# New issue orders for a one-core attention and gated-MLP kernel, with later loads of w_in's second half and of w_sp, and output block 12 in two column halves

## Chip, cores and metric

One NeuronCore of a Trainium2 chip. The metric is the device time of one execution in microseconds (us); lower is better. Times are medians of several runs.

## What is computed

Two pre-layernorm blocks on one sequence of 2048 tokens of width 448, in bf16. Attention has 16 heads of 28 and looks back over 8 positions, every second token. The second block gates one half of a hidden layer of 1792 with the other half, which is mixed over tokens by a 2048 x 2048 matrix.

```python
h  = x + A(layernorm(x));  h2 = h + B(layernorm(h))
def A(x):   # H=16, Dh=28, W=8, dilation 2
    q, k, v = split(x @ wqkv)
    logits = einsum('bhsd,bhswd->bhsw', q, k[idx]) * Dh**-0.5   # idx = s - 2*w, masked below 0
    return einsum('bhsw,bhswd->bhsd', softmax(logits), v[idx]) @ wo
def B(x):   # Fh = 896
    z = gelu(x @ w_in);  z1 = z[..., :Fh];  z2 = layernorm(z[..., Fh:])
    g = einsum('ts,bsf->btf', w_sp, z2) + b_sp[None, :, None]
    return (z1 * g) @ w_out
```

## The kernel before

Tokens are cut into 16 blocks of 128. A unit u is the pair of blocks u and u+8: both halves of the sequence lie on the two halves of TensorE's rows, so a "pair" of matmuls (s = 0, 1) runs side by side and takes two PSUM banks, one each. PSUM has eight banks, so at most four such pairs are in use.

Every piece of work is a named task, and the program is written from these:

- `bn1_b`, `rs1_u`, `nrm1_b`: layernorm 1 of a block or unit (L663 to L690). For units 0 to 2 a PE transpose `tT1_u` and an eviction `ev1_u` (L697 to L710) bring the result into `xh`; for units 3 to 7 a DMA transpose `tD1_u` on SP's queue does (L692). `bn2`, `rs2`, `nrm2`, `tD2_u` are the same for layernorm 2, all eight by DMA. They share the ring `tring` of four slots.
- `dp`, `rp` (L764, L650): the q and k weights, spread to the layout that the heads need. `mmq`/`mmk` and `evq`/`evk` (L807): q and k in three chunks of tokens; chunk 2 covers units 4 to 7, so `mmq2` and `mmk2` need `tD1_4` to `tD1_7`.
- nine attention tiles i of 114 tokens: `mmv` (L847) and `evv`; `mml` (L882, 64 small matmuls in four tasks); `exp` (ACT, L895); `mask` (DVE, L902); `mmr` (row sums, L911); `ln` and `rex` (ACT, L919 and L941); `mmo` (L931, 64 small matmuls); `ot` (DVE, L949). `mmo` waits for `ln` of its tile. Two tiles can hold an `E` buffer.
- per unit: `mmy` (output projection, L985), `h` (residual, L993), layernorm 2, `mmz2` (L1005, two halves k), gelu `ge` (L1027 or L1030; units 0 to 2 are first copied by `zr`), statistics `bn3`, `ag3`, `rs3` and `nrm3` (L1052).
- `mmz1_ch_f` and `gz1` (L1068, L1078): the other half of the hidden layer; needs `win0`, the second half of `w_in`. `win1` feeds `mmz2`. Each half comes as four DMAs on ACT's queue (L578).
- `g_tc_f` (L1105): the mixing over tokens, 16 matmuls of 512 columns; the first three (`g0_0` to `g0_2` in the orders) are cut into eight parts of two matmuls. They read `wsp0_b` (tokens 0 to 1023) or `wsp1_b`, transposed by DMA on SP's queue (L966). `ua`, `um` (DVE, L1115 and L1123) add the bias and multiply by z1; `wo_m` (L1134), `oa_m` (L1142) and the store `st_m` (L1146) finish a block.

The order on each engine and on SP's and ACT's DMA queues is a list written out in `ORDER` (L39 to L92). `Planner.run` walks the five lists with estimated durations; its clock decides which PSUM bank, ring slot or buffer a task gets, and where a table load is inserted: whenever a task asks for another activation table than the one loaded (L344). Waits are then derived from the data. `chain` (L1152) adds real waits that pace DMAs: load n of a list waits for step n-1 of another list. For w_in the chain is planned only (`False`); its place in ACT's list sets its issue.

```python
1160  chain(t_win[1] + t_win[0], [t_xh[NU - 1]] * 8, False)
1161  pace = [by[n % i] for i in range(4, NT) for n in ("exp%d_0", "mask%d", "ot%d")]
1163  chain([t_wsp[b][0] for b in S_ORDER], pace, depth=2)
1166  later = [t_bb, t_wout] + [t_wsp[b][1] for b in S_ORDER]
1167  chain(later, pace, depth=2)
```

The second `pace` (L1164) is ge4 to ge7, both halves, then the gz1_1 and ua0 tasks. So of `later`, w_out waits for ge4_0, wsp1_0 for ge4_1, wsp1_8 for ge5_0, wsp1_1 for ge5_1, wsp1_9 for ge6_0, and so on. `S_ORDER` is 0 8 1 9 ... 7 15.

Of the kernel before, what the change touches and what calls it, by code (L numbers as in the profile page):

```python
# [6 lines left out]
D = 448  # L7
# [33 lines left out]
        xhalo x0 x3 x11 x10 x1 x2 wqk1 x9 x14 x6 x7 x12 x13 x15 wv0 tD1_3 x4 x5 tD1_6 tD1_7 tD1_5 tD1_4 wsp0_0 wsp0_8  # L41
        tD2_0 wsp0_1 wsp0_2 wsp0_9 tD2_2 wsp0_10 tD2_1 tD2_3 wsp0_3 wsp0_11 wsp0_12 tD2_4 tD2_5 tD2_7 tD2_6 wsp0_13
        wsp0_4 bb wsp0_5 wsp0_6 wsp0_14 w_out wsp1_8 wsp0_15 wsp1_0 wsp0_7 wsp1_9 wsp1_10 wsp1_1 wsp1_2 wsp1_3 wsp1_4
        wsp1_11 wsp1_12 wsp1_5 wsp1_13 wsp1_6 wsp1_7 wsp1_14 wsp1_15 st1 st6 st7 st2 st5 st0 st3 st4 st10 st9 st8 st11
        st15 st13 st14 st12
""",
    "pool": """
        c_ident c_V c_nhalf c_mband c_kpad c_dup rs1_3 c_ones rs1_1 rs1_2 rs1_6 rs1_7 rs1_5 rs1_4 c_wo0 rs2_0 rs2_1
        rs2_2 rs2_3 rs2_4 rs2_5 rs2_7 rs2_6 rs3_5 rs3_2 rs3_1 rs3_3 rs3_0 rs3_7 rs3_6 rs3_4
""",  # L50
    "dve": """
        c_warm c_eps c_wkp c_xpad c_wqp bnh bn1_8 bn1_0 nrmh nrm1_0 bn1_3 nrm1_8 bn1_11 bn1_10 evh bn1_1 bn1_9 bn1_2
# [12 lines left out]
""",
    "act": """
        x8 wqk0 rsh rs1_0 wv1 rpk1 rpk0 rpk2 ev1_0 rpk3 rpq0 rpq1 rpq2 evk0_0 evk0_2 evq0_0 evq0_2 ev1_1 exp0_0 exp0_1
        evk1_3 evv0 evk1_2 evq1_2 ln0 rex0 evq1_1 evq1_0 evq1_3 wo1 evk1_0 wo3 win1_00 exp1_0 exp1_1 wo0 exp2_0 ln1
        exp2_1 evk2_0 wo2 rex1 win1_04 evk2_3 exp3_0 exp3_1 ln2 win1_10 ln3 rex3 rex2 evq2_0 win1_14 exp4_0 exp4_1
        win0_00 exp5_0 evv6 ln4 exp5_1 evv4 rex4 ln5 evv5 win0_04 exp6_0 rex5 exp6_1 zr0_1 exp7_0 ln6 exp7_1 evv8  # L70
        win0_10 rex6 ln7 rex7 exp8_0 exp8_1 win0_14 zr0_0 ln8 tab rex8 zr1_0 ge0_0 zr2_1 ge0_1 ge2_0 zr1_1 ge3_0 ge3_1
        ge1_0 gz1_0_1 ge1_1 gz1_0_5 gz1_0_4 ge2_1 gz1_0_0 ge5_0 ge5_1 gz1_0_6 ge4_0 ge7_0 ge4_1 gz1_0_2 gz1_1_5 ge6_1
        gz1_1_0 ge7_1 ge6_0 gz1_0_3 gz1_1_6 gz1_1_4 gz1_1_1 gz1_1_3 gz1_1_2
""",
    "pe": """
        warm dpk1 dpk0 tTh dpq0 dpk2 tT1_0 dpq1 dpk3 dpq3 mmk0_0 dpq2 mmk0_2 mmq0_0 mmq0_2 tT1_2 tT1_1 mml0_00 mml0_01
# [12 lines left out]
        g3_3_0 wo1_0 g3_2_0 g2_6_0 g3_0_0 g3_5_0 g2_4_0 g2_2_0 wo7_0 g2_3_0 wo5_0 wo6_0 g3_1_0 g2_0_0 wo0_0 wo3_0
        g2_1_0 wo4_0 g2_5_0 g3_6_0 wo10_0 wo8_0 wo9_0 wo11_0 wo15_0 wo13_0 wo13_6 wo15_6 wo14_0 wo14_6 wo12_0 wo12_6  # L90
# [128 lines left out]

class Task:  # L220
    __slots__ = ("name", "eng", "dur", "emit", "deps", "prio", "acq", "rel", "mode", "epoch",
                 "gate", "nbytes", "start", "end", "succ", "ndep", "rt", "nmm", "alts", "bw", "waits", "mark", "soft")

    def __init__(self, name, eng, dur, emit, deps=(), prio=0.0, acq=(), rel=(), mode=None,
# [14 lines left out]
        self.bw = 215.0  # L239
        self.waits = []  # L240
# [9 lines left out]
class Planner:  # L250
# [54 lines left out]
    def run(self, setup=1.6, t0=0.7):  # L305
# [15 lines left out]
        for _ in range(len(self.tasks)):  # L321
# [53 lines left out]
def bass_sequential_preLN__sliding_local_dilated__mixer_gmlp__prompt_kernel(  # L375
# [18 lines left out]
    with contextlib.ExitStack() as top:  # L394
# [816 lines left out]
```

The softmax here doesn't subtract the row's maximum and nothing guards it: scores larger than these inputs give would overflow.

## Time and profile before

| | |
|---|---|
| median of 5 runs | 258.35 us (257.66 to 258.9) |
| the profiled execution | 258.9 us, span 257.1 us |
| mean granted TensorE clock | 0.98 of full |
| start: PE's first matmul of weights (L764) | 7.18 us |
| first dense matmuls (L807) | 11.49 us |
| first mmz1 (L1068) | 104.5 us |
| first g (L1105) | 136.42 us |
| last matmul ends, span ends | 254.3 us, 257.1 us |
| landing of the 13 DMA transposes of tring | 2.9 to 7.4 us, median 3.2 |
| landing of the 32 wsp0 and wsp1 | 3.0 to 6.6 us, median 4.1 |
| landing of the 8 parts of w_in | 4.1 to 7.0 us, median 4.9 |

The span is from the first to the last instruction of the profiled execution; the time has some 1.8 us around it. In the chain of waits each piece is the work, or the transfer, that released the next. The slices cut the span into 40 equal parts of 6.43 us. A line of the program stands for all tasks that it emits (L650 and L652 are helpers for copies on ACT and DVE). "Busy" of PE counts a stretched run of matmuls as busy.

### The profile page before, as it was taken

The page shows a single profiled execution, that of the slowest core. Times are in us where ns is not written, and L with a number is a line of the kernel's source. Part 1 is how long each engine was busy: PE and PEld are TensorE (multiplying, and loading weights), DVE is VectorE, ACT ScalarE, POOL GpSimd, SP SyncE. Part 2 cuts the span into 40 slices and gives each one's busy share as a digit, 9 for nine tenths or more (in the row PEclk, how much of TensorE's full clock was granted, in tenths as well). Part 3 has the DMA queues.
Part 4 walks back from the last instruction along what each step waited for, and adds up shares of the span by engine and source line. Part 5 has one row for each costly group of instructions (what it writes and reads, how often), then busy time and mean ns, then how long its engine had stood idle before and what let it go on. Part 6 is the DMA issues. An engine that isn't in the chain of part 4 may idle for free.

```text
span 257.1 us, 6475 instructions
## 1 busy us (share of the span) xinstructions
PE 243.7 (95%) x2906; PEld 122.1 (47%) x2917; DVE 144.5 (56%) x281; ACT 89.7 (35%) x105; POOL 28.4 (11%) x72
## 2 busy tenths in 40 slices
PE   6899979989998899999999999999999999999995
PEld 2485543445565544444444444444444444444452
DVE  7986763676887877997695012055510204423753
ACT  3878644564865876776744000000000000000000
POOL 5403400001020102110723000000000000000000
PEclk9689997999999999999999999999999999999999
DMA  6970790234693955369999920005100000010112
GB/s 210 260 106 6 130 172 6 74 74 96 117 174 79 112 113 105 71 89 193 225 194 177 186 39 0 3 0 96 27 3 18 0 0 0 16 58 0 54 62 85
DMA packets 55412, 22.03 MB, mean 86 GB/s; under 512 B 46664, under 2 KB 55256, under 8 KB 55384
## 3 DMA queue, kind: packets, MB, share of 16 engines
q1 hardware_dynamic: 51952, 16.79, 36.1%
q10 hardware_dynamic: 3432, 4.82, 7.9%
q8 instruction: 23, 0.38, 0.7%
q14 instruction: 5, 0.04, 0.1%
HBM read 8.39 MB, written 1.84 MB: 40 GB/s over the span
## 4 chain that ended last, share of the span: by engine, by line
PE 86%; DMA 5%; ACT 4%; DVE 3%; issue 1%; ACTq 0%
PE psum L1105 37%; PE psum L807 11%; PE psum L1134 8%; PE psum L1068 8%; PE psum L1005 8%; PE psum L985 4%; PE psum L882 3%; PE psum L847 3%; DMA xh<-tring 3%; DMA z2p<-in_A_wqkv_dram 2%; PE psum L931 2%; ACT reg L650 2%; ACT reg L895 1%; PE psum L911 1%; DVE reg L902 1%; DVE reg L949 1%
## 5 line engine op out<-in xcount | busy, mean ns | idle before, releaser
L1115 DVE TENSOR_TENSOR ub<-psum,reg 128x512 bf16<-128x512 f32 x28 | 18.7, 687 | 58.7 <-PE psum L1105 58.4
L1105 PE MATMUL psum<-reg,z2p 128*128 128x512 bf16 x218 | 48.8, 379 | 0.3
L1105 PE MATMUL psum<-wspT_lo,z2p 128*128 128x512 bf16 x219 | 48.1, 379 | 0.4 <-issue 0.2
L1105 PEld LDWEIGHTS psum<-wspT_lo,z2p 128*128 128x128 bf16 x224 | 21.8, 98 | 26.6 <-DVE z2p L1052 0.4
L1105 PEld LDWEIGHTS psum<-reg,z2p 128*128 128x128 bf16 x224 | 21.9, 98 | 26.1
L807 PE MATMUL psum<-xh,reg 64*128 64x128 bf16 (+3 forms) x336 | 29.6, 330 | 2.1 <-DMA xh<-tring 1.9
L650 ACT ACTIVATE reg<-psum 128x896 bf16<-128x896 f32 (+5 forms) x26 | 20.8, 840 | 7.9 <-PE psum L807 5.2
L1005 PE MATMUL psum<-w_in,xh 64*128 64x448 bf16 x224 | 22.7, 349 | 0.5 <-DVE reg L949 0.5
L895 ACT ACTIVATE reg<-psum 128x928 bf16<-128x928 f32 x18 | 17.0, 944 | 15.9 <-PE psum L847 7.1
L1134 PE MATMUL psum<-reg 128*128 128x448 bf16 x112 | 22.3, 352 | 0.1
L1068 PE MATMUL psum<-xh,w_in 64*128 64x512 bf16 x196 | 21.8, 376 | 0.0
L807 PEld LDWEIGHTS psum<-xh,reg 64*128 64x128 bf16 x336 | 14.8, 104 | 12.6 <-DMA xh<-tring 2.0
L669 DVE BATCH_NORM_STATS2 st<-x_tm 128x6 f32<-128x448 bf16 x32 | 19.4, 607 | 1.0 <-DMA x_tm<-in_A_x_dram 0.9
L1142 DVE TENSOR_TENSOR tring<-psum,x_tm 128x448 bf16<-128x448 f32 x16 | 9.8, 621 | 18.0 <-PE psum L1134 18.0
L1036 DVE BATCH_NORM_STATS2 st<-z2p 128x6 f32<-128x448 bf16 x32 | 17.7, 610 | 3.9 <-ACT z2p L1030 3.9
L656 POOL TENSOR_TENSOR rs<-rs,nhalf 128x2 f32<-128x2 f32 x23 | 17.0, 738 | 2.0
L652 DVE CAST reg<-psum 128x1024 bf16<-128x1024 f32 (+3 forms) x11 | 12.0, 1095 | 9.1 <-PE psum L807 7.5
L655 POOL TENSOR_SCALAR rs<-mv 128x2 f32<-128x2 f32 x23 | 5.5, 239 | 105.2 <-DVE mv L670 86.4
L1078 ACT ACTIVATE reg<-psum 128x1024 bf16<-128x1024 f32 x14 | 13.9, 1025 | 7.4 <-PE psum L1068 7.4
L1134 PEld LDWEIGHTS psum<-reg 128*128 128x128 bf16 x112 | 11.0, 98 | 10.6
L902 DVE TENSOR_TENSOR reg<-reg,mband 128x1856 bf16<-128x1856 bf16 x9 | 10.1, 1125 | 9.8 <-ACT reg L895 9.8
L1005 PEld LDWEIGHTS psum<-w_in,xh 64*128 64x128 bf16 x224 | 10.6, 94 | 10.4 <-DVE reg L949 0.6
(68 smaller groups left out, 214.1 us busy)
## 6 DMA issues: line engine op xcount, KB each, us to landing
w_in<-in_B_w_in_dram ACTq DMA_DIRECT2D x4, 448.0 KB, 5.6
out_dram<-tring SPq DMA_DIRECT2D x16, 112.0 KB, 1.7
x_tm<-in_A_x_dram SPq DMA_DIRECT2D x15, 112.0 KB, 5.2
w_in<-in_B_w_in_dram ACTq DMA_DIRECT2D x4, 336.0 KB, 4.3
reg<-in_B_w_out_dram SPq DMA_DIRECT2D x1, 784.0 KB, 5.7
z2p<-in_A_wqkv_dram ACTq DMA_DIRECT2D x1, 672.0 KB, 5.9
reg<-in_B_b_sp_dram SPq DMA_DIRECT2D x1, 512.0 KB, 5.5
reg<-in_A_wqkv_dram ACTq DMA_DIRECT2D x1, 392.0 KB, 7.2
```

The source lines that it names most:

```text
L650: iss("act", lambda e: e.activation(dst, src, AF.Copy), reads=rd, writes=wr, after=after)
L656: iss("pool", lambda e: e.tensor_tensor(dst, dst, nh, ALU.pow), reads=rr + [r_nhalf], writes=rr)
L669: iss("dve", lambda e: e.bn_stats(st[:, b, :], x_tm[:, b, :]), reads=[r_x[b]], writes=[rl[b]])
L807: iss("pe", lambda e, c=c, s=s, gi=gi, lhs=lhs: e.matmul(psum[:, bk[s] * 512 + cw * gi:bk[s] * 512 + cw * gi + cw], lhs, xh[64 * s:64 * s ...
L895: iss("act", lambda e: e.activation(E[:, es[0], 2 * n:2 * n + 2, :], pair_view(lb, 0, 8 * JW), AF.Exp, scale=SCALE), reads=[r_bank[lb[0]], ...
L1005: iss("pe", lambda e, c=c, s=s: e.matmul(psum[:, zb[s] * 512:zb[s] * 512 + D], xh[64 * s:64 * s + 64, c, XO + 128 * u:XO + 128 * u + 128], ...
L1036: iss("dve", lambda e, b=b: e.bn_stats(st3[:, b, k, :], z2p[:, b, D * k:D * k + D]), reads=[r_z2[b][k]], writes=[r_st3[b][k]])
L1068: iss("pe", lambda e, c=c, s=s: e.matmul(psum[:, bk[s] * 512:bk[s] * 512 + 512], w_in[64 * s:64 * s + 64, c, 128 * f:128 * f + 128], xh[64 ...
L1078: iss("act", lambda e: e.activation(z1p[f].rearrange("p (s t) -> p s t", s=2)[:, :, 512 * ch:512 * ch + 512], pair_view(bk, 0, 512), AF.Ge ...
L1105: iss("pe", lambda e, b=b: e.matmul(psum[:, gb[0] * 512:gb[0] * 512 + 512], z2p[:, b, 128 * f:128 * f + 128], src[:, b, 512 * (tc % 2):512 ...
L1115: iss("dve", lambda e: e.tensor_tensor(ub[:, us_[0], :], psum[:, gb[0] * 512:gb[0] * 512 + 512], bb[:, 512 * tc:512 * tc + 512], ALU.add), ...
L1134: iss("pe", lambda e, f=f: e.matmul(psum[:, wb[0] * 512:wb[0] * 512 + D], z1p[f][:, 128 * m:128 * m + 128], w_out[:, f, :], start=(f == 0) ...
```

## The change

The five lists for SP, POOL, DVE, ACT and PE are replaced by new ones. The planned cost of a tD transpose goes from a rate of 200 and a fixed 1.6 us to 104 and 0.3; this is used for the assignment of buffers alone. `win0` is planned behind exp8_0. The steps that pace wsp0 begin at tile 7 where they began at tile 4, so its loads wait for exp7_0, mask7, ot7, exp8_0, mask8, ot8, h6, h7 and ge0_0 to ge3_0. Block 12 (`LAST_M`) is computed, added and stored as columns 0 to 223 and 224 to 447, each with its own PSUM bank. Of the orders, the parts for SP and ACT are whole below, those for DVE and PE cut.

```diff
@@ -38,56 +38,57 @@
 ORDER = {
     "sp": """
-        xhalo x0 x3 x11 x10 x1 x2 wqk1 x9 x14 x6 x7 x12 x13 x15 wv0 tD1_3 x4 x5 tD1_6 tD1_7 tD1_5 tD1_4 wsp0_0 wsp0_8
-        tD2_0 wsp0_1 wsp0_2 wsp0_9 tD2_2 wsp0_10 tD2_1 tD2_3 wsp0_3 wsp0_11 wsp0_12 tD2_4 tD2_5 tD2_7 tD2_6 wsp0_13
-        wsp0_4 bb wsp0_5 wsp0_6 wsp0_14 w_out wsp1_8 wsp0_15 wsp1_0 wsp0_7 wsp1_9 wsp1_10 wsp1_1 wsp1_2 wsp1_3 wsp1_4
-        wsp1_11 wsp1_12 wsp1_5 wsp1_13 wsp1_6 wsp1_7 wsp1_14 wsp1_15 st1 st6 st7 st2 st5 st0 st3 st4 st10 st9 st8 st11
-        st15 st13 st14 st12
+        xhalo x1 x0 x11 x9 x2 wqk1 x3 x10 x14 x15 x6 x7 wv0 x12 x4 x13 tD1_3 x5 tD1_4 tD1_7 tD1_6 tD1_5 tD2_1 tD2_0
+        wsp0_0 wsp0_8 tD2_3 tD2_2 tD2_4 wsp0_1 tD2_5 wsp0_2 wsp0_9 tD2_7 tD2_6 wsp0_10 bb wsp0_3 w_out wsp0_4 wsp0_11
+        wsp1_8 wsp0_5 wsp1_0 wsp0_12 wsp1_9 wsp0_6 wsp0_13 wsp1_1 wsp0_7 wsp0_14 wsp1_2 wsp0_15 wsp1_3 wsp1_10 wsp1_4
+        wsp1_11 wsp1_5 wsp1_12 wsp1_13 wsp1_14 wsp1_6 wsp1_15 wsp1_7 st7 st4 st5 st3 st8 st6 st0 st10 st9 st14 st13
+        st2 st12 st12b st1 st15 st11
 """,
     "act": """
-        x8 wqk0 rsh rs1_0 wv1 rpk1 rpk0 rpk2 ev1_0 rpk3 rpq0 rpq1 rpq2 evk0_0 evk0_2 evq0_0 evq0_2 ev1_1 exp0_0 exp0_1
-        evk1_3 evv0 evk1_2 evq1_2 ln0 rex0 evq1_1 evq1_0 evq1_3 wo1 evk1_0 wo3 win1_00 exp1_0 exp1_1 wo0 exp2_0 ln1
-        exp2_1 evk2_0 wo2 rex1 win1_04 evk2_3 exp3_0 exp3_1 ln2 win1_10 ln3 rex3 rex2 evq2_0 win1_14 exp4_0 exp4_1
-        win0_00 exp5_0 evv6 ln4 exp5_1 evv4 rex4 ln5 evv5 win0_04 exp6_0 rex5 exp6_1 zr0_1 exp7_0 ln6 exp7_1 evv8
-        win0_10 rex6 ln7 rex7 exp8_0 exp8_1 win0_14 zr0_0 ln8 tab rex8 zr1_0 ge0_0 zr2_1 ge0_1 ge2_0 zr1_1 ge3_0 ge3_1
-        ge1_0 gz1_0_1 ge1_1 gz1_0_5 gz1_0_4 ge2_1 gz1_0_0 ge5_0 ge5_1 gz1_0_6 ge4_0 ge7_0 ge4_1 gz1_0_2 gz1_1_5 ge6_1
-        gz1_1_0 ge7_1 ge6_0 gz1_0_3 gz1_1_6 gz1_1_4 gz1_1_1 gz1_1_3 gz1_1_2
+        x8 wqk0 rsh wv1 rpq1 rs1_0 rpk2 rpq0 rpq2 rpq3 ev1_0 rpk3 rpk0 rpk1 evq0_2 evq0_0 evk0_2 evk0_0 ev1_2 ev1_1
+        exp0_0 evv0 evk1_0 exp0_1 evq1_2 evq1_0 evq1_1 evk1_3 ln0 rex0 wo2 evv2 evk1_2 exp1_0 exp1_1 evk2_3 exp2_0 ln1
+        win1_00 exp2_1 wo1 wo3 rex1 wo0 ln2 exp3_0 win1_04 exp3_1 rex2 evk2_2 win1_10 evk2_1 ln3 exp4_1 win1_14 exp4_0
+        rex3 evv6 ln4 exp5_0 exp5_1 rex4 ln5 rex5 evv5 exp6_0 exp6_1 ln6 exp7_0 rex6 exp7_1 evv8 exp8_0 win0_00 zr0_1
+        exp8_1 ln7 zr1_1 win0_04 zr0_0 rex7 ln8 zr1_0 win0_10 rex8 ge0_1 ge0_0 ge3_0 win0_14 zr2_1 zr2_0 ge2_1 ge4_1
+        ge4_0 ge3_1 gz1_0_6 ge2_0 gz1_0_4 ge1_1 gz1_0_0 gz1_0_5 ge5_1 gz1_0_3 ge1_0 ge7_1 ge7_0 gz1_1_5 ge5_0 gz1_1_6
+        ge6_0 ge6_1 gz1_1_1 gz1_1_0 gz1_0_1 gz1_1_2 gz1_1_3 tab gz1_0_2 gz1_1_4
 """,
     "dve": """
...
-        nrm1_3 rpq3 nrm1_11 nrm1_2 nrm1_1 nrm1_10 nrm1_9 bn1_12 bn1_7 ev1_2 bn1_6 bn1_13 bn1_14 mask0 bn1_15 bn1_5
-        bn1_4 nrm1_6 nrm1_14 nrm1_7 nrm1_5 nrm1_15 nrm1_13 evk1_1 nrm1_4 nrm1_12 ot0 evv2 evv3 mask1 evv1 evq2_2 mask2
-        evk2_1 ot1 evq2_1 mask3 evq2_3 evk2_2 ot2 ot3 h0 bn2_0 bn2_8 mask4 h2 nrm2_0 nrm2_8 bn2_10 mask5 h1 bn2_1 ot4
-        bn2_2 bn2_9 evv7 h3 mask6 nrm2_2 nrm2_1 nrm2_10 ot5 bn2_3 nrm2_9 mask7 bn2_11 h4 ot6 zr2_0 bn2_12 mask8 nrm2_3
...
-        oa4 um3_2 ua3_5 ua3_6 um3_5 um3_6 oa8 oa10 oa9 oa11 oa15 oa13 oa14 oa12
+        c_warm c_wqp bnh c_eps c_wkp c_xpad bn1_8 bn1_1 nrmh bn1_0 evh bn1_11 nrm1_0 bn1_3 nrm1_8 bn1_9 bn1_2 nrm1_3
+        bn1_10 nrm1_1 nrm1_11 nrm1_9 nrm1_2 nrm1_10 bn1_4 bn1_7 bn1_12 bn1_6 bn1_15 bn1_14 nrm1_4 nrm1_12 nrm1_7
+        bn1_13 nrm1_6 nrm1_15 mask0 bn1_5 nrm1_14 evq1_3 nrm1_5 nrm1_13 evk1_1 ot0 evv1 mask1 evq2_2 evk2_0 evq2_0
+        mask2 evv3 ot1 evv4 evq2_1 evq2_3 mask3 ot2 h0 bn2_0 h1 mask4 bn2_9 bn2_8 ot3 bn2_1 mask5 nrm2_1 ot4 nrm2_9
+        nrm2_0 nrm2_8 evv7 h2 mask6 h3 ot5 bn2_2 bn2_3 bn2_11 bn2_10 mask7 ot6 h4 nrm2_3 nrm2_11 bn2_12 mask8 nrm2_2
+        bn2_4 nrm2_10 h5 nrm2_4 ot7 nrm2_12 bn2_13 bn2_5 h6 ot8 nrm2_5 bn3_0_0 h7 nrm2_13 bn2_7 bn2_15 bn2_6 bn2_14
...
+        um3_2 oa10 ua3_5 oa0 um3_5 ua3_6 um3_6 oa9 oa14 oa13 oa2 oa12 oa12b oa1 oa15 oa11
     "pe": """
-        warm dpk1 dpk0 tTh dpq0 dpk2 tT1_0 dpq1 dpk3 dpq3 mmk0_0 dpq2 mmk0_2 mmq0_0 mmq0_2 tT1_2 tT1_1 mml0_00 mml0_01
-        mmv0 mml0_10 mml0_11 mmk1_3 mmk1_2 mmq1_2 mmr0 mmq1_1 mmq1_3 mmo0_0 mmo0_1 mmq1_0 mmk1_1 mmo0_2 mmo0_3 mmk1_0
-        mmv2 mml1_00 mml1_01 mml1_10 mmv3 mml1_11 mmv1 mml2_00 mml2_01 mmq2_2 mmr1 mml2_10 mml2_11 mmk2_0 mmo1_0
-        mmo1_1 mmk2_1 mmo1_2 mmo1_3 mmk2_3 mml3_00 mml3_01 mmq2_1 mml3_10 mml3_11 mmr2 mmq2_3 mmo2_0 mmo2_1 mmr3
...
-        g2_1_0 wo4_0 g2_5_0 g3_6_0 wo10_0 wo8_0 wo9_0 wo11_0 wo15_0 wo13_0 wo13_6 wo15_6 wo14_0 wo14_6 wo12_0 wo12_6
+        warm dpq1 tTh dpk2 dpk0 dpq2 dpq0 dpq3 tT1_0 dpk3 dpk1 mmq0_2 mmq0_0 mmk0_2 mmk0_0 tT1_2 tT1_1 mmv0 mml0_00
+        mml0_01 mmq1_1 mmk1_0 mml0_10 mml0_11 mmq1_2 mmq1_0 mmk1_3 mmq1_3 mmr0 mmv2 mmo0_0 mmo0_1 mmk1_2 mmo0_2 mmo0_3
+        mmk1_1 mmv1 mml1_00 mml1_01 mmq2_2 mml1_10 mml1_11 mmk2_3 mml2_00 mml2_01 mmk2_0 mmr1 mml2_10 mml2_11 mmq2_0
+        mmo1_0 mmv3 mmo1_1 mmo1_2 mmk2_2 mmr2 mmo1_3 mmv4 mml3_00 mml3_01 mmq2_1 mml3_10 mml3_11 mmq2_3 mmo2_0 mmo2_1
+        mmk2_1 mmo2_2 mmo2_3 mmy0 mml4_00 mml4_01 mmr3 mml4_10 mml4_11 mmy1 mmo3_0 mmo3_1 mmo3_2 mmv6 mmo3_3 mmr4
+        mml5_00 mml5_01 mml5_10 mml5_11 mmv5 mmo4_0 mmo4_1 mmo4_2 mmr5 mmo4_3 mmv7 mml6_00 mml6_01 mmy2 mml6_10
+        mml6_11 mmo5_0 mmo5_1 mmy3 mmo5_2 mmr6 mmo5_3 mml7_00 mml7_01 mmv8 mml7_10 mml7_11 mmy4 mmo6_0 mmo6_1 mmo6_2
+        mmo6_3 mml8_00 mml8_01 mmz2_0_1 mmr7 mml8_10 mml8_11 mmz2_1_1 mmz2_0_0 mmo7_0 mmo7_1 mmy5 mmo7_2 mmr8 mmo7_3
+        mmz2_1_0 mmz2_3_0 mmo8_0 mmo8_1 mmy6 mmo8_2 mmo8_3 mmz2_3_1 mmz2_2_1 mmy7 mmz2_2_0 mmz2_4_1 mmz2_4_0 mmz1_0_4
+        mmz1_0_6 mmz1_0_0 mmz1_0_5 mmz2_5_1 mmz2_5_0 mmz1_0_3 mmz2_7_1 mmz1_1_5 mmz2_7_0 mmz1_1_6 mmz2_6_0 mmz1_0_1
+        mmz1_1_2 mmz2_6_1 mmz1_1_1 mmz1_1_0 mmz1_1_4 mmz1_1_3 mmz1_0_2 g0_2_0 g0_0_0 g0_1_0 g0_0_1 g0_2_1 g0_1_1
+        g0_1_2 g0_0_2 g0_2_2 g0_1_3 g0_0_3 g0_2_3 g0_0_4 g0_2_4 g0_1_4 g0_2_5 g0_0_5 g0_2_6 g0_1_5 g0_0_6 g0_1_6
+        g1_2_0 g0_3_0 g1_1_0 g0_2_7 g0_0_7 g1_5_0 g1_0_0 g1_4_0 g0_1_7 g1_6_0 g1_3_0 g0_4_0 g0_5_0 g2_6_0 g2_2_0
+        g3_1_0 g0_6_0 g2_4_0 g3_4_0 wo7_0 g2_3_0 g3_3_0 g2_1_0 wo6_0 wo4_0 g2_0_0 wo5_0 wo3_0 g3_0_0 g2_5_0 g3_5_0
+        wo10_0 g3_2_0 wo8_0 wo0_0 g3_6_0 wo14_0 wo9_0 wo14_6 wo13_0 wo13_6 wo2_0 wo12_0 wo12_6 wo1_0 wo12b_0 wo12b_6
+        wo15_0 wo15_6 wo11_0
...
@@ tD in ln_unit @@
-  rel=[("tr", h)], issue=1.3, bw=200.0)
+  rel=[("tr", h)], issue=1.3, bw=104.0, setup=0.3)
...
@@ output blocks @@
+                cols = [(0, D // 2), (D // 2, D)] if m == LAST_M else [(0, D)]
+                for ci, (c0, c1) in enumerate(cols):
+                    wb = []
...
-                            iss("pe", lambda e, f=f: e.matmul(psum[:, wb[0] * 512:wb[0] * 512 + D],
-                                                             z1p[f][:, 128 * m:128 * m + 128], w_out[:, f, :],
+                                iss("pe", lambda e, f=f: e.matmul(psum[:, wb[0] * 512:wb[0] * 512 + c1 - c0],
+                                                                 z1p[f][:, 128 * m:128 * m + 128], w_out[:, f, c0:c1],
...
@@ pacing @@
-        chain(t_win[1] + t_win[0], [t_xh[NU - 1]] * 8, False)
-        pace = [by[n % i] for i in range(4, NT) for n in ("exp%d_0", "mask%d", "ot%d")]
-        pace += [by["h6"], by["h7"]] + [by["ge%d_%d" % (u, k)] for u in range(3) for k in range(2)]
+        chain(t_win[1] + t_win[0], [t_xh[NU - 1]] * 4 + [by["exp8_0"]] * 4, False)
+        pace = [by[n % i] for i in range(7, NT) for n in ("exp%d_0", "mask%d", "ot%d")]
+        pace += [by["h6"], by["h7"]] + [by["ge%d_%d" % (u, k)] for u in range(4) for k in range(2)]
```

## Prediction

> **What bounds the kernel now.** I read the busy shares first, then the slices, the chain that ended last, and last the stretches of the chain that are not PE.
>
> The page of the kernel before, busy time and slices:
> ```profile
> PE 243.7 (95%) x2906; PEld 122.1 (47%) x2917; DVE 144.5 (56%) x281; ACT 89.7 (35%) x105; POOL 28.4 (11%) x72
> ...
> PE   6899979989998899999999999999999999999995
> ...
> PEclk9689997999999999999999999999999999999999
> DMA  6970790234693955369999920005100000010112
> ```
> PE is the bound. Before the last slice it is below 9 tenths, or at a low clock, only in the first 14 (to 90 us), and its last idle gap ends at 98.75, so only there can a new order win anything. From 136.42 to 254.28 us the chain is PE without a gap (117.9 us of L1105 and L1134); the change computes the same there. 257.1 - 243.7 = 13.4 us of PE idle is nearly all the room there is, and the start (up to 7.2 us) and the tail (2.8 us) hold some 6 of it.
>
> The chain of waits around the one DMA on it after the start:
> ```profile
> 29.34 1.28 PE psum L807 x14
> 30.63 0.36 PE psum L847 x5
> 30.99 7.36 DMA xh<-tring
> 38.34 0.04 issue
> 38.39 2.93 PE psum L807 x14
> 41.31 0.52 PE psum L911 x6
> 41.83 0.49 PE psum L882 x24
> 42.33 1.62 PE psum L807 x14
> ```
> PE waits for tD1_4, the last transpose of layernorm 1, which took 7.36 us to land. The 14 matmuls right after it took 2.93 us, the same 14 at 42.33 took 1.62.
>
> Stretches of the same execution (fields: stretch, length, PE busy, and third from the end the granted clock):
> ```profile
> 36.00:38.39 2.39, 0.52 (x37) 0.37 (x34) 2.05 (x2) 1.25 (x2) 0.00 (x0) 1.00 1.19 189
> 38.39:41.31 2.92, 2.92 (x22) 0.89 (x22) 0.08 (x1) 0.00 (x0) 0.00 (x0) 0.55 0.12 35
> ```
> The stall is 1.87 us of idle PE and then 2.9 us at a granted clock of 0.55: 1.87 + (2.93 - 1.62) = 3.2 us in all. The Trainium skill ("TensorE: Matmul & The Clock Gate", Part 1) puts the drop to half clock after an idle window of about 3.4 us; by that alone a 1.87 us gap would cost 1.87. The row decides: 3.2.
>
> Why 7.36 us? In the timeline tD1_4 is issued on SP at 30.99, and win1_00 (448 KB of w_in) on ACT at 31.16. tD1 pairs that met no such load landed in 3.0 to 3.3 us.
>
> **The change, part by part.**
>
> *Start, to mmq2_2.* Before, the first dense group starts at 11.49, after three rpk on ACT (2.54 us for 3 from 7.61), ev1_0 and rpk3. After, ACT runs rpq1, rs1_0, rpk2, rpq0, rpq2, rpq3, ev1_0: 7.61 + 4 x 0.85 + 0.51 (rs1: 0.30 + 0.21) + 0.49 + 0.81 = 12.8, so 1.4 us later. Part of it comes back: stepping the new PE order with the rows' durations I reach mmq2_2 at 34.4 to 35.7, with 2.2 us less done before it (mmv3 1.45, four mml halves 0.78) than at 36.52 before: between 0.1 earlier and 1.4 later. I take **0.4 us lost**, the low side, since the row for the old order holds small waits that the stepped one has not.
>
> *tD1_5 in place of tD1_4.* Win1_00 moves on ACT from before exp1_0 to after ln1. Before mmq2_2, DVE now ends with mask0 (released by exp0_1 near 24.6), bn1_5 0.76, nrm1_14 0.45, evq1_3 (ready when mmq1_3 ends near 27.9; 0.95), nrm1_5 and nrm1_13 0.9: tD1_5 goes out near 29.9 and lands at 33.1 with 3.2 us, 1.3 us or more ahead of need. win1_00 goes out only after ln1, near 41. **3.2 us gained**; with the 7.4 us landing it would be 37.3, about 2 late, and nothing is gained.
>
> *Tile stretch (41.3 to the first mmz1).* Before, PE idles 0.72 + 0.32 + 0.25 + 0.28 + 0.44 + 1.14 + 0.50 + 0.63 = 4.28 us there. Runs of small matmuls are also stretched. From the chain of waits:
> ```profile
> 85.76 1.43 PE psum L1005 x14
> 87.19 1.44 PE psum L882 x63
> 88.63 1.43 PE psum L1005 x14
> ```
> 63 took 1.44 where 32 take 0.39 (59.53, 63.54): the second 32 cost 0.66 more than their own 0.39. Six such runs sum to 2.8. So 7.1 us lost before. After, I step tile by tile with exp 0.94, mask 1.13, mmr 0.40, ln 0.94, rex 0.97, ot 1.24, h 1.06, bn2 0.76, mm 1.62, mmy 1.63, mmz2 1.36 to 1.43, mmv 1.45, and 0.1 to 0.2 between engines. PE waits 0.25 at mmy1 (h0 frees its banks), 0.5 at mmr4, 1.5 at mmr5 (exp5_1, then mask5 behind ot3 and bn2_1 on DVE), 0.45 at mmr6, 0.6 for banks at mmv8 and mml8_10, and 0.5 at mmz2_3_0: 3.8. Small runs side by side (mml4 with mmr3, mmr4 with mml5, mml6 with mmo5, mmo5_3 with mml7, mmo6 with mml8: the last 96 in a row, 1.3) add 3.5, of which 1.1 falls into waits already counted: 2.4. 7.1 - 6.2 = **0.9 gained** (3.3 if no run is stretched; -1.2 if each of seven waits for masks is 0.3 longer).
>
> *Transposes tD2.* tD2_3 goes out 5 us before mmz2_3_0 (landing 2.9 to 7.4 in the rows, beside win0_04: the 0.5 above), tD2_2 and tD2_4 6.6 and 7.6 us before their use, which hides them.
>
> *Second half of w_in.* Issue times on ACT move from 57-90 us to after exp8_0. The last, win0_14, stands behind ge3_0. Counted from the end of mmz2_3_0, ACT still has zr1_0, rex8, a table load of 1.28 and ge0_1, ge0_0: issue at +4.0, landing (4.1 to 7.0) at +8.1 to +11.0. PE does mmo8, mmy6, five mmz2 and mmy7 and half of mmz1_0_4 first: +11.4. Hidden; without that cover, 1 us per us.
>
> *w_sp transposes.* Their waits move from exp4..ot8 to exp7..ge3. In SP's queue wsp1_8 (waits for ge5_0) now stands ahead of wsp0_5, 12, 6, 13, 7, 14 and 15, and g0 waits for those. From the end of mmz1_1_5: ge5_0 done at +4.4, ten issues of 1.3 us, wsp0_14 landing at +20.2 (4.1) to +22.7 (6.6). PE has eight mmz1 (12.1), three mmz2 (4.1) and 17 parts of g0 (7.5) first: +23.6. Hidden, by 0.9 at worst.
>
> *tab.* It now stands after gz1_1_3, and since it asks for the exp set, two more table loads come (1.28 each by the row at 95.67, where the next ACTIVATE starts at 96.96). Behind them wait gz1_0_2, gz1_1_4 and wsp1_13; nothing needs these for 9 us: nothing. The Trainium skill ("ScalarE: Activation LUTs", What ACT_TABLE_LOAD costs) counts 2.66 us a switch with a drain; the row shows no drain, and 5.3 us would still be hidden.
>
> *Block 12 in halves.* 14 matmuls of 224 columns for 7 of 448 (1.32 us): half the columns each, but a weight load (98 ns) per matmul: 14 x 0.098 = 1.37, so 0.05 to 0.1 more; one more add and one more store on idle DVE and SP. And it is not the last block: the new orders end with wo11, oa11, st11, whole. The tail stays as it is (add 0.62, store 1.7 to landing). **0.1 lost.**
>
> POOL's and the other moves only follow these; PE's work is otherwise equal.
>
> **Sum:** -0.4 + 3.2 + 0.9 - 0.1 = 3.6 us faster: the profiled execution's 258.9 (span 257.1 and 1.8 around it) becomes 255.3. The median of the runs, 258.35, lies 0.55 lower: 254.75, say **254.7**.
>
> **Rivals.**
> - *The tile stretch gains more.* Small runs ride in PE's queue unstretched (the 32 at 59.53 took 0.39): 2.4 more, and the start costs nothing: 6.4 gained, 252.0. Against it: the 1.44 row.
> - *tD1_5 is late as well* (mask0 and evq1_3 hold DVE, or wo2 collides): the 3.2 goes, 257.9; about no change, since the split block is not the last.
> - *Slower: the w_in pieces collide with tD2.* Moved to the end of attention, win0_04 to win0_14 go out between tD2_3, tD2_2 and tD2_4, which PE now needs within 5 to 8 us. One collision before cost 3.2 us with the clock. Two of that size, at mmz2_3_0 and at mmz1_0_4, cost 6.4: 261.1. It decides once they cost over 3.6 together. For it: a 7.1 us landing of the tD2 issued at 82.24, beside w_in; against it: filler mmz2 and mmy work in between.
>
> **How the numbers follow.** Forecast 0.52, more gain 0.22, tD1_5 late 0.14, collision 0.12. The forecast's own range, with the tile bounds, is 252.3 to 256.8. The range 251.5 to 258.0 takes in the first two cases and most of the third, leaving out some 0.2. This kernel's measurement can tell about 0.3% (0.8 us) from no change. Faster: 0.50 + 0.22 + 0.04 = 0.76; same: 0.02 + 0.09 + 0.01 = 0.12; slower: 0.12.
>
> **What would show it.** Right: no DMA on the chain near 31 us and no slice below 9 in PEclk after 20 us; the first L807 near 12.9; four table loads; the first L1105 near 132.7; an unsplit block last. Wrong: a wait of PE on xh<-tring or w_in before 110 us, on wspT_lo at the start of L1105, or several L911 waits over 1 us.

## The result, and the profile after

The changed kernel takes 256.19 us (median of 45 runs), the kernel before 257.5 us (median of 87). The ratio is 0.9969, with a 95% interval of 0.9954 to 0.9983: a gain of 0.3%, some 0.8 us, where 1.4% was forecast. It leaves out executions over 1.5% slower than the fastest of their kernel, as some of the kernel before are, and so lies nearer to 1 than the two medians do. The profiled execution of the changed kernel took 255.52 us, with a span of 253.7 us. Lines have moved, up to L1068 by 14: L807 is now L821, L1005 is L1019, L1068 is L1082, L650 is L664. L1105 is L1120, L1134 is L1153, L1142 is L1162.

The page of the changed kernel, busy time and slices:
```profile
PE 243.6 (96%) x2914; PEld 124.4 (49%) x2924; DVE 142.0 (56%) x280; ACT 93.4 (37%) x109; POOL 28.9 (11%) x72
...
PE   7499999999999999999999999999999999999995
...
PEclk9979999999999999999999999999999999999999
```
The low clock in the seventh slice is gone. What is left lies in the second and third slices: the start.

The chain of waits of the changed kernel, where the transpose stood before:
```profile
30.90 0.29 PE psum L945 x32
31.18 1.28 PE psum L821 x14
32.47 1.45 PE psum L861 x28
33.92 0.39 PE psum L896 x31
34.31 0.28 issue
34.59 1.45 PE psum L821 x11
```
PE reaches mmq2_2 at 34.31 and starts it at 34.59. The 0.28 us of "issue" is most likely a wait for the last transpose, tD1_5: issued at 29.39, it landed at 34.51. It took 5.1 us, not the 3.2 of the prediction, so of the forecast 1.3 us to spare nothing was left in this execution. PE's waits from 20 us to the first mmz1 are down to three short ones (columns: total us, times, longest):
```profile
PE psum L925 <- DVE reg L916: 0.6, 2, 0.5
PE psum L821 <- issue: 0.3, 1, 0.3
PE psum L896 <- DVE reg L666: 0.2, 1, 0.2
```
The first mmz1 starts at 103.61, the first g at 133.03 (before, read the same way: 104.35 and 136.42). Set against the one profile of before, it went as forecast: 258.9 to 255.52 us, 3.4 gained where 3.6 was expected. Against the runs, only about a quarter of it is there.

The chain of waits at the start of the changed kernel:
```profile
4.21 5.51 DMA x_tm<-in_A_x_dram
...
9.74 0.64 DVE st L683
...
10.59 0.40 DVE tring L699
...
11.04 0.58 PE psum L714 x7
...
11.64 0.93 ACT xh L664
...
12.61 4.63 PE psum L821 x112
```
Layernorm 1 of the first unit is late. `bn1_3` waits for x3, which has moved from second to seventh of the x blocks and weights on SP's queue and lands at 9.7 us, and `nrm1_8`, which the first transpose needs, stands behind `bn1_3` on DVE. PE is idle for 1.8 us before L714, and the first dense matmuls then run at a low clock, as the next experiments show beside a full one.

### The profile page after: what moved, and what is told of

The parts are those of the page before. It is cut to its first block, busy times and chain, and to the rows that moved or that the text cites. A ratio compares the mean times of both kernels' runs of the same rounds, so it can differ in the third digit from the quotient of the medians.

```text
span 253.7 us, 6508 instructions
## 1 busy us (share of the span) xinstructions
PE 243.6 (96%) x2914; PEld 124.4 (49%) x2924; DVE 142.0 (56%) x280; ACT 93.4 (37%) x109; POOL 28.9 (11%) x72
## 4 chain that ended last, share of the span: by engine, by line
PE 82%; DVE 8%; ACT 3%; DMA 2%; POOL 1%; SPq 1%; issue 1%; POOLq 0%
PE psum L1120 38%; PE psum L821 10%; PE psum L1153 8%; PE psum L1019 6%; PE psum L999 5%; PE psum L861 4%; PE psum L896 4%; PE psum L1082 3%; DVE st L1050 3%; PE psum L945 2%; DMA x_tm<-in_A_x_dram 2%; ACT reg L909 1%; DVE reg L916 1%; DVE z2p L1066 1%; DVE reg L963 1%
## 5 line engine op out<-in xcount | busy, mean ns | idle before, releaser
L1120 PE MATMUL psum<-reg,z2p 128*128 128x512 bf16 x219 | 48.9, 379 | 0.3
L1120 PE MATMUL psum<-wspT_lo,z2p 128*128 128x512 bf16 x219 | 48.2, 379 | 0.4 <-DVE z2p L1066 0.2
L1120 PEld LDWEIGHTS psum<-wspT_lo,z2p 128*128 128x128 bf16 x224 | 21.8, 98 | 26.6 <-DVE z2p L1066 0.4
L1120 PEld LDWEIGHTS psum<-reg,z2p 128*128 128x128 bf16 x224 | 21.9, 98 | 26.2
L821 PE MATMUL psum<-xh,reg 64*128 64x128 bf16 (+3 forms) x336 | 28.1, 321 | 0.9 <-ACT xh L664 0.5
L1019 PE MATMUL psum<-w_in,xh 64*128 64x448 bf16 x224 | 22.9, 349 | 0.0
L664 ACT ACTIVATE reg<-psum 128x896 bf16<-128x896 f32 (+5 forms) x26 | 20.5, 829 | 4.7 <-PE psum L778 2.5
L1153 PE MATMUL psum<-reg 128*128 128x448 bf16 (+1 forms) x119 | 22.2, 341 | 0.0
L1082 PE MATMUL psum<-xh,w_in 64*128 64x512 bf16 x196 | 22.1, 376 | 0.0
L821 PEld LDWEIGHTS psum<-xh,reg 64*128 64x128 bf16 x336 | 14.5, 102 | 10.0 <-ACT xh L664 1.0
L669 POOL TENSOR_SCALAR rs<-mv 128x2 f32<-128x2 f32 x23 | 6.3, 272 | 99.0 <-DVE mv L684 80.9
L1153 PEld LDWEIGHTS psum<-reg 128*128 128x128 bf16 x119 | 11.6, 98 | 9.9
L1162 DVE TENSOR_TENSOR tring<-psum,x_tm 128x448 bf16<-128x448 f32 (+1 forms) x17 | 9.8, 593 | 11.9 <-PE psum L1153 9.5
L1019 PEld LDWEIGHTS psum<-w_in,xh 64*128 64x128 bf16 x224 | 10.9, 94 | 9.8 <-issue 0.4
L1082 PEld LDWEIGHTS psum<-xh,w_in 64*128 64x128 bf16 x196 | 9.5, 94 | 11.3
```

Of the source, the lines that this page charges most:

```text
L664: iss("act", lambda e: e.activation(dst, src, AF.Copy), reads=rd, writes=wr, after=after)
L821: iss("pe", lambda e, c=c, s=s, gi=gi, lhs=lhs: e.matmul(psum[:, bk[s] * 512 + cw * gi:bk[s] * 512 + cw * gi + cw], lhs, xh[64 * s:64 * s ...
L1019: iss("pe", lambda e, c=c, s=s: e.matmul(psum[:, zb[s] * 512:zb[s] * 512 + D], xh[64 * s:64 * s + 64, c, XO + 128 * u:XO + 128 * u + 128], ...
L1082: iss("pe", lambda e, c=c, s=s: e.matmul(psum[:, bk[s] * 512:bk[s] * 512 + 512], w_in[64 * s:64 * s + 64, c, 128 * f:128 * f + 128], xh[64 ...
L1120: iss("pe", lambda e, b=b: e.matmul(psum[:, gb[0] * 512:gb[0] * 512 + 512], z2p[:, b, 128 * f:128 * f + 128], src[:, b, 512 * (tc % 2):512 ...
L1153: iss("pe", lambda e, f=f: e.matmul(psum[:, wb[0] * 512:wb[0] * 512 + c1 - c0], z1p[f][:, 128 * m:128 * m + 128], w_out[:, f, c0:c1], star ...
```

## Experiments

Each was timed beside the kernel before, which had medians of 256.2 to 257.5 us from one group of runs to the next; a small step between two ratios is therefore not sure. **"Before + ..." starts from the old kernel, "after + ..." from the changed one.** Executions of one kernel differ in their mean granted clock, in steps of some 0.0066 (of 257 us that is 1.7 us lost, or 3.4 us at half clock), so some comparisons below are made between executions of the same mean clock. That is a help and no exact measure: one step costs 0.7 to 1.9 us in the groups of these runs.

**1. The kernel before, unchanged.**

> The kernel before, unchanged, to see how its executions differ. My theory: the wait for the last layernorm-1 transpose and the low clock behind it differ from execution to execution; the profiled one (258.9 us, clock 0.980) had them in full and is not typical. Then the clocks of the executions spread over several steps (0.980, 0.987, 0.993), the time falls with the clock, and a new profile shows a gap ahead of the first 512-column matmuls of less than 1 us or no low clock after it. Rival: every execution pays the 3.2 us; then nearly all are at clock 0.980 and the new profile has a gap of 1.5 to 2 us again. Both: ratio 1.000.

Measured: 257.86 against 256.7 us, ratio 1.0033 (0.9994 to 1.0073). The span of the profile is 254.2 us instead of 257.1. Its waits of PE from 28 to 42 us, and a stretch after the wait (fields as in the prediction):
```profile
PE psum L807 <- DMA xh<-tring: 1.8, 1, 1.8
```
```profile
36.00:39.50 3.50, 2.55 (x56) 1.24 (x58) 1.93 (x3) 1.24 (x2) 0.00 (x0) 1.00 0.44 89
```
The wait for tD1_4 is there again, 1.8 us, but the clock behind it is 1.00, where it was 0.55. The start differs as well. Two stretches (6.43 to 12.86 and 12.86 to 19.29 us) of the profile the prediction was made from, then of this one:
```profile
6.43:12.86 6.43, 5.31 (x54) 2.86 (x56) 5.79 (x18) 5.25 (x7) 2.69 (x10) 0.62 1.12 259
12.86:19.29 6.43, 6.24 (x166) 5.20 (x162) 5.56 (x15) 4.57 (x8) 0.60 (x1) 0.85 0.74 106
```
```profile
6.43:12.86 6.43, 4.53 (x86) 2.74 (x84) 5.98 (x18) 6.27 (x9) 3.27 (x10) 1.00 1.06 245
12.86:19.29 6.43, 5.48 (x176) 4.13 (x172) 5.62 (x15) 3.92 (x6) 0.46 (x2) 1.00 0.89 111
```
In the first, PE waited 1.6 us for the q and k weights and the stretch has a clock of 0.62; in the second it had no such wait and the clock was full, and its first dense matmuls started at 10.43 instead of 11.49. Of 100 executions of the kernel before, 29 had a mean clock of 1.000 (mean 255.6 us), 31 one of 0.992 to 0.993 (257.5), and only 5 one of 0.98 (260.0), like the one profiled.

**2. Before + one move: win1_00 goes out after ln1.**
```diff
-... evk1_0 wo3 win1_00 exp1_0 exp1_1 wo0 exp2_0 ln1
+... evk1_0 wo3 exp1_0 exp1_1 wo0 exp2_0 ln1 win1_00
```


> The kernel before with one move: the first w_in DMA (win1_00) goes out after ln1, as in the changed kernel, and not ahead of exp1_0. The other parts are old. My theory (the stall is there in only some executions): 0.5 to 1.8 us faster (ratio 0.993 to 0.998), and the times of single runs lie closer together. Rival (it is paid every time): 3 us faster (0.988).

Measured: 254.13 us, ratio 0.9944 (0.9908 to 0.998). PE doesn't wait for a transfer there; mmq2_2 starts at 34.97. The forecast of this run allowed 0.5 to 1.8 us and its rival 3: at a mean clock of 1.000 it is 1.7 us faster than before (253.85 us in 5 executions, 255.57 in 29). One task moved in one list gives as much as the whole change or more.

**3. After + win1_00 back to its early place,** ahead of exp1_0.

> The changed kernel with win1_00 put back ahead of exp1_0. In the changed kernel the last transpose (tD1_5) goes out near 29.3 us and the DMA would follow near 31.7. My theory: 0 to 1.8 us slower than the changed kernel (ratio to before 0.997 to 1.004). Rival: the full 3 us slower (1.009). If tD1_5 is through before the w_in data come, no difference.

Measured: 255.63 us, ratio 0.9994 (0.9966 to 1.0022), against 0.9969 for the changed kernel: the intervals overlap, and at equal clocks the two take nearly the same (256.45 and 256.46 us at 0.987, 255.48 and 255.70 at 0.993). In the new orders tD1_5 is issued by 30.7 us and win1_00 only at 31.07, so it meets the transpose in the last part of its way at most; tD1_5 landed in 3.0 us. Either of the two (run 3: the load 1.6 us behind the transpose; run 2: the load behind ln1) does away with the collision.

**4. Before + the moves of the title alone:** win0 behind exp8_0, wsp0 paced from tile 7 and, in SP's list, placed behind tD2_0 and tD2_2, with bb, w_out and some of wsp1 moved too (the lines for SP are left out here); the other orders are old.
```diff
-... exp4_1 win0_00 exp5_0 ... evv5 win0_04 exp6_0 ... evv8 win0_10 rex6 ... exp8_1 win0_14 zr0_0 ...
+... exp8_0 win0_00 exp8_1 win0_04 zr0_0 ln8 tab rex8 win0_10 zr1_0 ge0_0 zr2_1 ge0_1 win0_14 ge2_0 ...
-        pace = [by[n % i] for i in range(4, NT) for n in ("exp%d_0", "mask%d", "ot%d")]
+        pace = [by[n % i] for i in range(7, NT) for n in ("exp%d_0", "mask%d", "ot%d")]
```


> The kernel before with only the moves that the change is named for: win0 behind exp8_0, exp8_1, rex8 and ge0_1 on ACT, the w_sp transposes paced from tile 7 on and placed behind tD2 on SP; all other orders old, no halves. If the gain lies in freeing the attention from those transfers: 1 to 2 us faster. My reading of the profiles, that PE did not wait for them there: within 0.8 us of before; if the last part of w_in comes after the first mmz1, 1 to 2 us slower with PE waiting for it near 104 us.

Measured: 260.62 us, ratio 1.0172 (1.0119 to 1.0225). Its chain of waits, and a stretch of it:
```profile
30.16 8.51 DMA xh<-tring
...
38.71 3.17 PE psum L807 x11
...
42.97 2.39 PE psum L807 x14
```
```profile
38.40:45.00 6.60, 6.29 (x68) 2.27 (x68) 1.50 (x2) 1.89 (x2) 0.00 (x0) 0.54 0.00 0
```
win1_00 is issued at 30.33, 0.17 us behind tD1_4, which takes 8.51 us; PE idles for 3.0 us, and then 6.6 us at a clock of 0.54 follow. These moves don't help by themselves. Run 10 splits the loss.

**5. After + the old order of the start** (x on SP, the first tasks on POOL, DVE, ACT and PE), all else new. Cut, for PE:
```diff
-        warm dpq1 tTh dpk2 dpk0 dpq2 dpq0 dpq3 tT1_0 dpk3 dpk1 mmq0_2 mmq0_0 mmk0_2 mmk0_0 tT1_2 tT1_1 mmv0 mml0_00
+        warm dpk1 dpk0 tTh dpq0 dpk2 tT1_0 dpq1 dpk3 dpq3 mmk0_0 dpq2 mmk0_2 mmq0_0 mmq0_2 tT1_2 tT1_1 mmv0 mml0_00
```


> The changed kernel with the old order of the start (all up to the 128-column q and k matmuls and the transposes tT1_2 and tT1_1, on every engine). My theory: the new start costs what the order gains later, by a later first dense matmul (12.6 us against 10.4 to 10.7 in two profiles of the old start at full clock) and a low clock in the 3 to 7 us after it. Then this kernel starts dense work near 10.7, most executions show a mean clock of 0.999 to 1.000, and the ratio to before is 0.984 to 0.990 (2.5 to 4 us). Rival: the start's loss is given back anyway, since the last transpose sets the pace, and the tile orders are what loses: ratio 0.994 to 0.998, as for the changed kernel.

Measured: 253.71 us, ratio 0.9889 (0.9832 to 0.9945). The first dense matmuls start at 10.58, the first g at 130.28. The new start is the part of the change that loses. Of the forecast clocks one half failed: four of the six executions still have a mean clock of 0.993.

**6. Before + win1_00 late (2) + the new start.** The reverse.

> The kernel before with win1_00 behind ln1 (0.9944 of before) and the new order of the start. My theory: 1.8 to 3 us slower than with the old start (ratio to before 1.001 to 1.006), mean clock 0.987 to 0.993 in nearly all executions. Rival (the start doesn't matter): 0.994, and the clocks as before.

Measured: 257.41 us, ratio 1.0022 (0.9988 to 1.0056), against 0.9944 without the new start. The first dense matmuls start at 13.09 (10.73 in run 2), the first g at 133.75 (131.53).

**7. Before + win1_00 late + block 12, which is the last there, in halves,** with the code of the change.

> The kernel before with win1_00 behind ln1 and block 12, there the last block in all orders, in two column halves as in the change. The last add falls from 0.62 us to some 0.36, and the last store moves half the bytes in rows of 448 bytes; 14 matmuls in place of 7 cost 0 to 0.1 us. Mine: the stretch from the last matmul to the end of the span falls from 2.8 to about 2.5 us, ratio to before 0.993. Rival: rows under 512 bytes make the store land later, the stretch stays at 2.8 or grows.

Measured: 255.35 us, ratio 0.9936 (0.9904 to 0.9967): nothing won over run 2. From the last matmul to the end of the span it takes 3.9 us, 2.8 in run 2. The end of its chain:
```profile
249.49 0.40 DVE tring L1162
249.89 0.02 issue
249.91 1.60 DMA out_dram<-tring
...
251.63 0.39 DVE tring L1162
```
The second half's add waits until the first half's store has landed. Each half is meant to write its own columns of the ring slot, but the emitted function reads `cols` when it runs, and by then the loop over the blocks has left it with the one entry of the last `m`. So each add counts as writing the whole slot. The rival, that half stores land later, is not what it shows: they landed in 1.60 and 1.53 us, whole ones near the end in some 1.7. In the changed kernel the same wait is there, 2.3 us on DVE, for st12; there oa11 still starts as its matmuls end (250.89 and 250.91), and the wait costs nothing.

**8. After + five unused matmuls of ones ahead of tT1_0.** They fill PE's wait for layernorm 1; their result isn't read.
```diff
-        warm dpq1 tTh dpk2 dpk0 dpq2 dpq0 dpq3 tT1_0 dpk3 ...
+        warm dpq1 tTh dpk2 dpk0 dpq2 dpq0 dpq3 warm2 tT1_0 dpk3 ...
```


> The changed kernel with five more matmuls of ones (results unused) ahead of tT1_0, in the gap of 1.8 us in which PE waits for layernorm 1 of unit 0. It splits the start's loss in two. If it is mostly the low clock after that gap: most executions at 0.999 to 1.000, and 1 to 1.7 us faster than the changed kernel (ratio to before 0.990 to 0.993), with the first dense matmuls still near 12.6 us. If it is only the later start: no change (0.997), or slower by as much as the five delay tT1_0 (up to 0.5 us).

Measured: 255.21 us, ratio 0.9933 (0.9896 to 0.997). The first 4.6 us of dense matmuls in the changed kernel, then here:
```profile
12.60:17.20 4.60, 4.59 (x113) 4.49 (x114) 4.50 (x13) 3.57 (x6) 1.21 (x3) 0.69 0.64 111
```
```profile
12.60:17.20 4.60, 4.39 (x134) 3.95 (x132) 4.50 (x13) 4.12 (x8) 1.02 (x3) 1.00 0.59 121
```
The same length of time holds 134 matmuls instead of 113. Six of its twelve executions now have a mean clock of 1.000, where one of 46 of the changed kernel had. At the lower clock of 0.993 the two kernels take the same (medians 255.6 and 255.5), so what run 8 gains is clock, and not an earlier start (12.42 here, 12.61 in the changed kernel). So a good part of the start's loss is the clock after its gap.

**9. Run 5 + halves on block 11, the true last, `cols` bound at its definition.**
```diff
-        LAST_M = 12
+        LAST_M = 11
...
-                    def em(m=m, wb=wb, ts_=ts_, c0=c0, c1=c1, ci=ci):
+                    def em(m=m, wb=wb, ts_=ts_, c0=c0, c1=c1, ci=ci, cols=cols):
```


> The changed kernel with the old start (0.9889 of before), and with the halves moved to block 11, which is the last in its orders, and the writes of each half's add bound to that half alone. In the changed kernel, and in the run with block 12 as the last block, the second half's add waited for the first half's store (2.3 and 1.75 us): the list of columns is read when the tasks are emitted, after the loop has gone on to block 15, so each add is taken to write the whole slot. Mine: with the writes bound, no wait of an add on a store there; from the last matmul to the end of the span 2.5 us in place of 2.8; ratio 0.987 to 0.989. Rival: the wait is a full ring of slots, not the halves; then it stays, and the stretch is 4 us as with block 12 last.

Measured: 253.22 us, ratio 0.9826 (0.9777 to 0.9874), the lowest ratio of all. The end of its chain, in a span of 251.6 us:
```profile
245.94 3.25 PE psum L1153 x24
249.18 0.02 issue
249.21 0.39 DVE tring L1162
```
From the last matmul's end to the end of the span it takes 2.4 us, 2.8 in the changed kernel. The ratio's interval overlaps that of run 5, and at a clock of 1.000 both take 252.7 us (3 and 2 executions): the 0.4 us at the end is seen in this row and not shown by the times.

**10. Run 4 + win1_00 late.**

> The run with only the late loads (1.0172 of before) and win1_00 behind ln1. If its loss was all at the transpose tD1_4 (8.5 us to land, 3.0 us of PE idle, then 6.6 us at a clock of 0.54): ratio 0.994 to 0.997, about that of win1_00 alone. If the late loads themselves cost (PE waited 2.3 us for ot7 at 94.9 us there): 1.000 to 1.004.

Measured: 256.67 us, ratio 0.9982 (0.9947 to 1.0017), against 0.9944 for win1_00 alone. The stall at tD1_4 is gone, but a wait of PE in the tile stretch stays (as in run 4):
```profile
PE psum L1005 <- DVE reg L949: 2.3, 1, 2.3
```
The trace tells what releases it. The matmuls are mmz2_1_0, which need tD2_1: it landed at 81.86 us, 7.4 us before PE goes on at 89.30. What ends just before is ot7 on DVE, at 89.16, whose result mmz2_1_0 doesn't read. So the wait is for PSUM banks that ot7 frees. `Planner.run` gives them to mmz2_1_0 here, while in run 2 it gives it others. With the old orders the late loads lose a little, and what this wait costs comes by the assignment of banks and not from a transfer; the changed kernel's own orders have no such wait.

**11. Run 5 + 2 and 2 unused matmuls in the start's two gaps.**

> The changed kernel with the old start and two pairs of extra matmuls of ones (unused) in its two gaps, ahead of dpk3 and of mmk0_0. With the old start 4 of 6 executions still showed one low-clock window (0.993, 254.0 us) and 2 none (1.000, 252.7). If windows come from thin work in 7 to 12 us: nearly all at 0.999 to 1.000, near 252.8 us, ratio 0.982 to 0.988. If the window is decided elsewhere: clocks and ratio as with the old start alone (0.989).

Measured: 253.2 us, ratio 0.9837 (0.9793 to 0.9882). All its six runs have a clock of 1.000, 252.76 to 253.82 us, but at that clock it takes 253.3 us where run 5 takes 252.7. The low clock goes (in run 5 two of six executions had 1.000), and the fillers cost some 0.6 us themselves, a small sample: they wait for a bank that ACT frees, and the first dense matmuls start at 11.06 instead of 10.58.

**12. After + x3 directly behind x0 on SP.**

> The changed kernel with one DMA put back: x3 goes out on SP right after x0 and not after wqk1. In the changed kernel nrm1_8 stands on DVE behind bn1_3, which waits until 9.7 us for x3, and tT1_0, ev1_0 and the first dense matmuls wait for nrm1_8. Mine: that wait ends near 7 to 8 us, PE's gap ahead of tT1_0 falls from 1.8 us to under 0.8, the first dense matmuls come at 11.6 to 12.2 us in place of 12.6 (ACT's six rp copies and rs1_0 are then the bound), and a part of the executions lose a low-clock window: ratio to before 0.991 to 0.996. Rival: the lateness is ACT's order alone; then the first dense matmuls stay at 12.6 and the ratio at 0.997.

Measured: 255.4 us, ratio 0.9946 (0.9908 to 0.9984), against 0.9969: a miss in its main point. The wait for x3 is gone, but the first dense matmuls start at 13.11 in its profile and not at 11.6 to 12.2. PE's waits from 6 to 14 us, and the longest in total of its weight loads there:
```profile
PE psum L778 <- ACT reg L664: 2.4, 1, 2.4
PE psum L821 <- ACT xh L664: 0.2, 1, 0.2
```
```profile
PEld psum L778 <- DMA z2p<-in_A_wqkv_dram: 3.5, 2, 2.7
```
The wait moved, and not to ACT, to which the first row puts it down. The matmul is dpq3, which needs wqk1, the last part of the q and k weights. The edit put wqk1 behind x3 on SP: it was issued 0.5 us later and landed at 10.64 instead of 7.79 us, and dpq3's weight load starts at 10.68. `rpk2`, whose end at 8.73 released dpq3 in the changed kernel, had ended at 9.08. The clock is low from there on as well: tT1_0's seven matmuls take 0.88 us, 0.58 in the changed kernel. So the run took one late transfer away and made another late, and it can't tell x3 from ACT's new order. An estimate from the changed kernel's rows: its copies on ACT ahead of ev1_0 end at 10.77 and ev1_0 starts at 11.64, so the wait for x3 is worth at most 0.9 of the some 2 us by which the new start is late; the rest would lie ahead of it on ACT. At equal clocks (0.987 and 0.993) the kernel is 0.8 and 0.95 us faster than the changed one.

## Why the prediction was wrong

The time, 256.19, lies in the range; the gain, 0.3% instead of 1.4%, is not what was forecast. That the range holds is in part luck: the kernel before itself came out at 257.5, 0.85 us under the 258.35 that the sum started from. All signs named for being right came true: no DMA on the chain near 31 us, no slice below 9 in PEclk after 20 us, the first dense matmuls at 12.61 (12.9 forecast), four table loads, the first g at 133.03 (132.7 forecast), an unsplit block last. But all of them were set against one execution of the kernel before, and that execution was not a usual one. The rival of a later tD1_5 (257.9) and the collision at tD2 (261.1) didn't happen: after 20 us PE idles for a transfer at mmq2_2 alone, for at most 0.28 us.

**The step that failed is "I take 0.4 us lost", the start.** The comparison was with a start that isn't the usual one: its 11.49 holds a 1.6 us wait for the q and k weights and a low clock, and in run 1 the same kernel starts its dense work at 10.43, at full clock. Reckoned as the prediction does it, PE reaches mmq2_2 at 34.31 with 2.2 us less done, which makes 36.5: as early as the 36.52 of the execution first profiled, but 1.3 us later than run 1, where PE got there at 35.19. The 12.9 came near by luck: the copies on ACT ended at 10.77 and not at 12.0, and the wait of `bn1_3` for x3, moved from second to seventh, which was not in the stepping at all, put 0.9 us back. The new start comes 2.0 to 2.4 us later (12.61 against 10.58 in run 5, 13.09 against 10.73 in run 6). Where executions of the same mean clock are compared it costs 1.3 us (256.2 against 254.95 us, runs 6 and 2, at 0.993) to 1.7 us (255.7 against 254.0, the changed kernel and run 5, at 0.993). On top of that it brings a stretch at low clock: 45 of 46 executions of the changed kernel have a mean clock of 0.987 or 0.993, where 29 of 100 of the kernel before have 1.000. By the medians, clock and all, the new start costs 2.5 us (256.19 against 253.71, run 5) to 3.3 us (257.41 against 254.13, runs 6 and 2).

**"3.2 us gained" at tD1_4** had the right place and cause (runs 2 and 4), but it was mis-sized too: it measured 1.7. The 1.87 us of idle PE is paid in both profiles of before (1.9 and 1.8), and run 2 wins this term. The other, 1.31 us of low clock, came in one profile and not in the other. Here the Trainium skill ("TensorE: Matmul & The Clock Gate", Part 1), which the prediction set aside for its row, was nearer to run 1: the drop follows an idle window of some 3.4 us, and a gap of 1.8 us left the clock at 1.00. The same section calls that window free-running, so that what an execution meets depends on where in the window it falls. That the mean clocks fall into steps of 3.4 us at half clock fits; that a gap shorter than it can end in the low clock, as in the execution first profiled, is not what it states. The prediction also read that transposes without a load behind them landed in 3.0 to 3.3 us; one of the three in that stretch took 3.66, and the changed kernel's last took 5.11, which used up the time to spare.

**"0.9 gained" in the tile stretch** was about right, as far as the runs tell: the changed kernel with the old start (run 5) is 1.1 us below run 2 at a clock of 1.000 (252.72 against 253.85, 2 and 5 executions), and starts g 1.25 us earlier (130.28 and 131.53). This step holds all other parts of the change as well. PE's waits for masks fell from 2.1 us to 0.6 (L911, now L925).

**The halves** cost next to nothing in their place, as said. The step counted "one more add and one more store on idle DVE and SP" and missed that the add waits for the store (2.3 us); run 7 shows it where it counts. An unsplit block ends the kernel, as said.

**The hidden steps** held: four table loads, 1.28 us each, and no wait for w_in or for w_sp.

The sum by the runs, at equal clocks: 1.7 for the stall and 1.1 for the tiles, less 1.3 to 1.7 for the start, is 1.1 to 1.5 us gained. Set side by side at equal clocks, the two kernels differ by 1.75 us (0.993) and 2.1 us (0.987), so the parts agree with the whole only roughly. The changed kernel's mean clock, 0.989 by its 46 executions, lies under the 0.993 of before's 100, and this takes a part of the gain back: over all these executions the means are 256.26 and 257.20, 0.94 us apart.

What stays open: why a gap of 1.8 us is followed by the low clock in some executions only, and how the lateness of the new start divides between x3 and ACT's order.

## What to carry to other kernels

One profiled execution can lie at the end of its kernel's spread: before a term is taken from it, set its time and clock against the runs, and don't count a term that is clock as sure. Signs that are read from a profile can all come true while the gain against the runs does not. When orders are rewritten whole, test the parts one at a time: here one load moved by a few places was worth as much as all of it or more, and the change did best with its start put back (runs 5, 9 and 11). Of a stepped order, check first which tasks wait for an input that has moved back in its queue, and after moving one transfer, look at what now stands behind it.

## What the runs showed of the hardware

- The mean granted clock of an execution falls mostly into steps, near 1.000, 0.993, 0.987 and 0.980 (90 of the 100 executions of the kernel before; the other ten lie at 0.998 or 0.999), and in that kernel the times go with it: 255.6, 257.5, 258.6 and 260.0 us. With unused matmuls in the start's gaps, executions at 1.000 rose from 1 of 46 to 6 of 12 (run 8, a gap of 1.8 us) and from 2 of 6 to 6 of 6 (run 11, gaps of 0.5 and 0.6 us).
- A DMA transpose with a 448 KB load issued 0.2 us behind it from another queue took 7.25 to 8.51 us to land (three profiles). Where the load came later, the last transpose of that stretch took 2.9 to 5.1 us (eleven profiles; 4.83 in run 2, 5.11 in the changed kernel). The load behind ln1 was worth 1.7 us at equal clock (run 2).
- One place in a DMA queue can count for far more than its issue: wqk1, put out 0.5 us later behind one block of x, landed 2.85 us later (10.64 and 7.79 us, run 12 and the changed kernel).
- Two table loads back to back on ACT took 2.57 us in the changed kernel, with no drain to be seen between them or behind them.
